# 160 no-operations on TensorE ahead of the first product, and the later ones laid out anew

## The chip, the core and the metric

The kernel runs on one core of one Trainium2 chip. Its five engines are called here PE (TensorE, the matrix products; PEld is its loading of the stationary operand), DVE (VectorE), ACT (ScalarE), POOL (GpSimd) and SP (SyncE, which issues all DMAs). Each works through its own program in order and meets the others at semaphores. The metric is device time in microseconds (us), the median of several executions.

## What is computed

The reference is a causal retention layer followed by a feed-forward layer with softplus:

```
scores = (q @ k.T) / sqrt(64)              # 8 batches, 8 heads, 576 positions, head size 64
ret    = scores * gamma_h ** (i - j)       # for i >= j, else 0
x      = (ret @ v) as 4608 tokens x 512
h      = x @ w_in                          # 512 -> 2048
out    = softplus(h) @ w_out               # 2048 -> 512, all in float32
```

## The kernel before

Retention is done in chunks of 128 tokens and pairs of heads, with a running state between chunks. The feed-forward part takes the tokens in units of 512. Its float32 products are split into high and low parts and are done as three products each, 128x128 by 128x512 ("large products" below). The weights, for the two later passes also some sums of them, pass through a ring of eight buffers that SP fills by DMA.

The program has these stretches on PE.

- **The opening.** PE begins with three products that multiply a tile of ones (`fill`, written by DVE) into a bank that nobody reads (`idle`, L800). Then the retention of the first eight steps is done in an order written out by hand (`BEGIN`): S is the scores of a step (L414), U its sums (L430), V its values (L454), X the part from the state (L462); K and O are DVE's masking and scaling, C the scaling of the values on ACT. SP's first DMAs bring `first` (two parts) and then `whole`, one for each step. The hidden layer's first products stand at L541.
- **The layers' products** (L541, L570, L581, L584, L917, L1053, L1064): large products one behind another, 12 or 6 in a row on one weight block.
- **The chunk runs.** At 33 places between the layers' products `chunk_products` puts the retention of one chunk: up to 128 small 64x64 products, those of scores (L236), sums (L252), values (L340) and states (L352) mixed in a fixed order.

After each chunk run a number is taken from the table `PADS` (its key is the number of the run). `pad()`, called behind each large product of L541, L917 and L1053, then puts out at most `PAD` = 2 no-operations at a time until this number is used up. A no-operation (NOP) reads and writes nothing; its one effect on the program is that all later PE instructions stand that many places further on. PE's instructions come to the core by DMA, in a queue of their own (q8 in the profile).

Of the kernel before, what the change touches and what calls it, by code (L numbers as in the profile page):

```python
# [101 lines left out]
SUM_WORK = ('f2 x3 p4', '', '', 'a0', 'u0 p5', 'u1', '', 'f3', 'p6', 'k0 c0', '', 'v0 v1', 'g0 p7', '', 'g1', '')  # L102
GROUPS = {1: (4, None), 4: (5, 4), 8: (6, 5), 12: (7, 6), 15: (8, 7)}
ODD = 12
PADS = {2: 6, 3: 74, 4: 64, 5: 6, 6: 8, 10: 14, 11: 108, 12: 68, 16: 10, 17: 70, 18: 48, 20: 52, 22: 50, 24: 50, 26: 18, 28: 10, 29: 70, 30: 24}
PAD = 2
LOADS = {1: (10,), 2: (11,), 4: (12, 13), 8: (14, 15), 12: (16, 17), 15: (18, 19)}
SCALES = {3: (10, 11), 7: (12, 13), 11: (14, 15), 14: (16, 17)}
# [14 lines left out]
def retention_softplus_ffn(ctx: ExitStack, tc, first, whole, others, consts, w, out):  # L123
    nc = tc.nc
# [240 lines left out]
    def chunk_products(steps, done, values_first=False):  # L365
# [32 lines left out]
        runs[0] += 1  # L398
        pads[0] = PADS.get(runs[0], 0)

# [395 lines left out]


    idle = ps_val.tile([P, 2, T], F32, tag="val", name="idle")
    for n in range(OPENING):
        nc.tensor.matmul(idle[:, 0, 0:2 * C], fill[:, 0:P], fill[:, 0:2 * C], start=True, stop=True)  # L800

# [637 lines left out]
```

## Time and profile before

| what | value |
|---|---|
| median of 3 runs | 810.11 us (808.95 to 810.88) |
| profiled execution, its own time | 808.12 us |
| profiled execution, span of the trace | 806.4 us |
| PE busy | 799.9 us (99%) |
| PE's share of the chain that ended last | 95% |
| NOPs on PE | 750 |
| PE waits for another engine or a DMA, all rows | 3.4 us |

The time of an execution is the span and some 1.7 us around it. The span runs from the first to the last instruction of any engine. The chain that ended last is the list of work, each piece released by the one before, that leads to the last instruction: an engine that holds 95% of it sets the time, and what the other engines do counts only where PE waits.

### The profile page before, as it was taken

What the parts mean: (1) busy time and instruction counts of PE and PEld (TensorE: products, weight loads), DVE (VectorE), ACT (ScalarE), POOL (GpSimd) and SP (SyncE); (2) the same over time, 40 slices, a digit from 0 to 9 for tenths busy, and PEclk for the clock granted to TensorE, in tenths of its full rate; (3) what the DMA queues carried; (4) which work ended last, traced back from release to release, by engine and by line L of the source; (5) the groups of instructions that cost most, each with busy time, mean ns of one, the idle gap of its engine ahead of it and who ended that gap; (6) DMA issues with size and microseconds to landing.
All of it is one profiled execution on the core that took longest, in us unless ns stands there. A gap on an engine that the chain in (4) does not pass through costs nothing.

```text
span 806.4 us, 19457 instructions
## 1 busy us (share of the span) xinstructions
PE 799.9 (99%) x7292; PEld 659.1 (82%) x7292; DVE 585.9 (73%) x987; ACT 395.3 (49%) x698; POOL 120.9 (15%) x213
## 2 busy tenths in 40 slices
PE   8999999999999999999999999999999999999998
PEld 6788888878888888888888888888888888888887
DVE  5988868788779986777679965546589934335785
ACT  6878763344533363343445654343255734434543
POOL 4322132212221220222111001122100000000000
PEclk9999999999999999999999999999999999999999
DMA  9989989998995779898977678777656675555564
GB/s 359 382 326 318 313 286 363 321 358 294 366 362 209 276 281 384 277 322 263 322 260 234 218 245 256 230 250 252 215 179 215 222 247 195 192 191 194 194 220 158
DMA packets 100457, 216.77 MB, mean 269 GB/s; under 512 B 11152, under 2 KB 11408, under 8 KB 100368
## 3 DMA queue, kind: packets, MB, share of 16 engines
q1 hardware_dynamic: 100368, 215.54, 77.6%
q8 instruction: 61, 1.00, 0.5%
q14 instruction: 28, 0.23, 0.1%
HBM read 174.60 MB, written 40.89 MB: 267 GB/s over the span
## 4 chain that ended last, share of the span: by engine, by line
PE 95%; DVE 2%; DMA 2%; POOL 0%; issue 0%; ACT 0%; SPq 0%; DVEq 0%
PE acc L917 22%; PE sum L1053 20%; PE two L917 14%; PE two L1053 6%; PE y L570 5%; PE h L541 5%; PE y L581 5%; PE third L252 3%; PE acc L1053 2%; PE third L1053 2%; PE y L1053 2%; PE two L236 2%; PE two L340 2%; PE third L917 2%; PE two L352 2%; DMA raw<-whole 1%
## 5 line engine op out<-in xcount | busy, mean ns | idle before, releaser
L917 PE MATMUL acc<-xt,ring 128*128 128x512 f32 x792 | 199.7, 389 | 0.0
L917 PEld LDWEIGHTS acc<-xt,ring 128*128 128x128 f32 x792 | 148.4, 188 | 31.6 <-ACT g L1093 0.3
L1053 PE MATMUL sum<-parts,ring 128*128 128x512 f32 x708 | 170.9, 392 | 0.0
L1047 DVE TENSOR_TENSOR parts<-g,parts 128x512 fp32r<-128x512 f32 x196 | 134.2, 694 | 47.1 <-ACT parts L1043 44.3
L1043 ACT CAST parts<-g 128x512 fp32r<-128x512 f32 x196 | 121.1, 622 | 73.5 <-DVE parts L1047 27.3
L1053 PEld LDWEIGHTS sum<-parts,ring 128*128 128x128 f32 x708 | 131.6, 188 | 27.8
L917 PE MATMUL two<-xt,ring 128*128 128x512 f32 x504 | 128.0, 389 | 0.0
L917 PEld LDWEIGHTS two<-xt,ring 128*128 128x128 f32 x504 | 94.4, 188 | 20.1 <-DVE held L1332 0.4
L1072 ACT ACTIVATE g<-g 128x512 f32<-128x512 f32 x84 | 52.8, 629 | 68.6 <-DVE g L1087 40.4
L1087 DVE TENSOR_TENSOR g<-two,g 128x512 f32<-128x512 f32 x28 | 19.4, 691 | 83.1 <-PE two L917 83.1
L229 POOL TENSOR_TENSOR qv<-qv,consts_sb 128x256 f32<-128x256 f32 x58 | 48.8, 844 | 128.4 <-DMA qv<-others 128.4
L1085 ACT COPY g<-acc 128x512 f32<-128x512 f32 x28 | 16.5, 589 | 95.5 <-PE acc L917 95.5
L1053 PE MATMUL two<-parts,ring 128*128 128x512 f32 x216 | 50.5, 389 | 0.0
L581 PE MATMUL y<-g,wout 128*128 128x512 f32 x192 | 47.6, 395 | 0.0
L1053 PEld LDWEIGHTS two<-parts,ring 128*128 128x128 f32 x216 | 40.5, 188 | 8.5
L541 PE MATMUL h<-xt,win 128*128 128x512 f32 x192 | 46.4, 391 | 0.0
L570 PE MATMUL y<-wout,g 128*128 128x512 f32 x180 | 44.1, 393 | 0.0
L1129 ACT ACTIVATE g<-acc 128x512 f32<-128x512 f32 x28 | 16.7, 597 | 53.3 <-PE acc L917 53.3
L541 PEld LDWEIGHTS h<-xt,win 128*128 128x128 f32 x192 | 35.9, 188 | 8.0 <-DVE win L671 0.4
L581 PEld LDWEIGHTS y<-g,wout 128*128 128x128 f32 x192 | 35.4, 188 | 7.9 <-DVE g L556 0.3
L570 PEld LDWEIGHTS y<-wout,g 128*128 128x128 f32 x180 | 33.3, 188 | 7.4 <-ACT g L552 0.3
L294 DVE TENSOR_TENSOR a<-two,mask 128x512 f32<-128x512 f32 x32 | 22.0, 687 | 20.8 <-PE two L352 17.7
(171 smaller groups left out, 1260.7 us busy)
## 6 DMA issues: line engine op xcount, KB each, us to landing
ring<-split SPq DMA_DIRECT2D x116, 256.0 KB, 4.6
ring<-combined SPq DMA_DIRECT2D x112, 256.0 KB, 3.5
ring<-outcombined SPq DMA_DIRECT2D x112, 256.0 KB, 3.0
ring<-outsplit SPq DMA_DIRECT2D x84, 256.0 KB, 3.4
qv<-others SPq DMA_DIRECT2D x58, 320.0 KB, 4.8
wst<-w SPq DMA_DIRECT2D x32, 512.0 KB, 6.4
keys<-others SPq DMA_DIRECT2D x58, 256.0 KB, 5.0
split<-win SPq DMA_DIRECT2D x16, 512.0 KB, 6.6
```

Of the source, the lines that this page charges most:

```text
L229: nc.gpsimd.tensor_mul(v, v, f.unsqueeze(2).broadcast_to([P, 4, D]))
L252: mm = nc.tensor.matmul(L["T"][rows[h ^ s], t, part[s]], L["kp"][rows[t], s, rows[h]], L["v"][rows[t], s, rows[h]], start=True, stop=True, ...
L294: nc.vector.tensor_mul(a[:, :, at], src.rearrange("p h (s c) -> p h s c", c=HC), mask.unsqueeze(1).unsqueeze(1).broadcast_to([P, 2, 2 * le ...
L541: nc.tensor.matmul(h, tile_of(wins[p], a, kt), xt[:, b, T1 + half, kt % 2], start=(n == 0), stop=(n == 3 * NKT - 1))
L570: nc.tensor.matmul(ys[u][tt], g[:, a, tt * P:(tt + 1) * P], wouts[p][:, :, b], start=p == 0 and n == 0, stop=False)
L581: nc.tensor.matmul(ys[u][tt], tile_of(wouts[p], a, tt), g[:, b], start=u == 1 and p == 2 * MIXED and n == 0, stop=n == 2, skip_group_check ...
L917: nc.tensor.matmul(bank, w[:, ta, kt * P:(kt + 1) * P], xt[:, tb, x, kt], start=start and k == 0, stop=k == 5, skip_group_check=True)
L1043: nc.scalar.copy(t[:, HI], g_slot(J, n))
L1047: nc.vector.tensor_sub(t[:, LO], g_slot(J, n), t[:, HI].bitcast(F32))
L1053: nc.tensor.matmul(bank[m], w[:, a, m * P:(m + 1) * P], t[:, b], start=start and n == 0, stop=n == 2, skip_group_check=True)
L1072: nc.scalar.activation(c, c, AF.Softplus)
L1087: nc.vector.tensor_add(c11, y, c11)
```

## The change

The table `PADS` gets a new key 0 with 160, and `160` NOPs are put out in one unbroken row ahead of the three `idle` products. The entries for the chunk runs are replaced: 750 NOPs behind large products become 964. In all, PE has 1124 instead of 750. Nothing else is changed: products, tiles, waits and the programs of the other engines stay as they are.

```
-PADS = {2: 6, 3: 74, 4: 64, 5: 6, 6: 8, 10: 14, 11: 108, 12: 68, 16: 10, 17: 70, 18: 48, 20: 52, 22: 50, 24: 50, 26: 18, 28: 10, 29: 70, 30: 24}
+PADS = {1: 4, 2: 92, 3: 92, 4: 14, 5: 2, 6: 30, 7: 48, 9: 70, 10: 108, 13: 66, 14: 58, 15: 32, 17: 42, 19: 8, 20: 70, 21: 26, 23: 52, 25: 46, 27: 52, 29: 52, 0: 160}
...
     idle = ps_val.tile([P, 2, T], F32, tag="val", name="idle")
+    for n in range(PADS.get(0, 0)):
+        nc.tensor.nop(hint="pad", nofuse=True)
     for n in range(OPENING):
         nc.tensor.matmul(idle[:, 0, 0:2 * C], fill[:, 0:P], fill[:, 0:2 * C], start=True, stop=True)
```

On PE, at the start of the program, there stood before (`part` is what the DMAs of `first` bring, `raw` what those of `whole` bring; a loading of the stationary operand goes with each product and is not listed):

```order
L1433 UNCONDITIONAL_BRANCH
L800 MATMUL idle<-fill 128x256 x3
L414 MATMUL pair_215<-part_106 64x128 x4
L414 MATMUL pair_215<-part_106 64x64 x4
L430 MATMUL bank<-part_107 64x64 x4
L454 MATMUL bank<-a_whole,part_107 64x128 x4
```

and there stands now:

```order
L1435 UNCONDITIONAL_BRANCH
L800 NO_OP x160
L802 MATMUL idle<-fill 128x256 x3
L414 MATMUL pair_215<-part_106 64x128 x4
L414 MATMUL pair_215<-part_106 64x64 x4
L430 MATMUL bank<-part_107 64x64 x4
L454 MATMUL bank<-a_whole,part_107 64x128 x4
```

All of PE's products now stand behind 160 NOPs, the three on `fill` too.

On PE, behind the second chunk run, the hidden layer's products (`win` is a block of w_in) stood before with six NOPs in three pairs:

```order
L541 MATMUL h<-xt,win_750 128x512
L406 NO_OP x2
L541 MATMUL h<-xt,win_750 128x512
L406 NO_OP x2
L541 MATMUL h<-xt,win_750 128x512
L406 NO_OP x2
L541 MATMUL h<-xt,win_750 128x512 x9
```

and stand now with a pair behind each of them (92 in all after this run); the first of these rows are:

```order
L541 MATMUL h<-xt,win_914 128x512
L406 NO_OP x2
L541 MATMUL h<-xt,win_914 128x512
L406 NO_OP x2
L541 MATMUL h<-xt,win_914 128x512
L406 NO_OP x2
L541 MATMUL h<-xt,win_914 128x512
L406 NO_OP x2
```

The products keep their order; only pairs of NOPs have come between more of them here, and between fewer behind other runs.

## Rows read from the trace of the kernel before

**Rows 1.** The page: span, engines (busy us, share, instructions), instruction queue, chain by engine.

```profile
span 806.4 us, 19457 instructions
...
PE 799.9 (99%) x7292; PEld 659.1 (82%) x7292; DVE 585.9 (73%) x987; ACT 395.3 (49%) x698; POOL 120.9 (15%) x213
...
q8 instruction: 61, 1.00, 0.5%
...
PE 95%; DVE 2%; DMA 2%; POOL 0%; issue 0%; ACT 0%; SPq 0%; DVEq 0%
```

**Rows 2.** Timeline of PE, 0 to 9.5 us: start, length, what, [idle before <-releaser].

```profile
1.53 2.93 PE L800 MATMUL idle<-fill 128*128 128x256 f32 x6 [1.53 <-DVE fill L777]
4.39 0.92 PE L414 MATMUL pair<-part 64*64 64x128 f32 x16
5.47 1.08 PE L430 MATMUL bank<-part 128*64 128x64 f32 x7 [0.16 <-ACT part L232]
...
7.96 0.56 PE L414 MATMUL pair<-raw 64*64 64x128 f32 x16 [0.44 <-DMA raw<-whole]
9.23 0.45 PE L414 MATMUL pair<-raw 64*64 64x128 f32 x8 [0.72 <-DMA raw<-whole]
```

**Rows 3.** Waits of PE, then of PEld: total us, times, longest.

```profile
PE idle L800 <- DVE fill L777: 1.5, 1, 1.5
PE pair L414 <- DMA raw<-whole: 1.2, 2, 0.7
...
PEld pair L414 <- DMA raw<-whole: 2.0, 4, 0.9
```

**Rows 4.** The chain that ended last, to 28 us: start, length, what.

```profile
0.82 0.38 SPq L201
...
2.19 7.00 DMA raw<-whole
9.19 0.04 issue
9.23 0.56 PE pair L414 x16
...
18.44 0.69 DVE win L671
...
25.07 1.87 POOL raw L229 x2
```

**Rows 5.** NOPs of line 406: all; stretches 72.338:72.345 and 72.408:72.415 (same answer but start); 72.33:73.16.

```profile
L406 PEldq NOP  x750: 13/13/13, 48.1 to 552.8; - x188
...
L406 PEldq NOP  x1: 13/13/13, 72.3 to 72.3; - x1
...
L406 PEldq NOP  x1: 13/13/13, 72.4 to 72.4; - x1
...
L406 PEldq NOP  x11: 13/13/13, 72.3 to 73.1; - x11
```

**Rows 6.** The chain that ended last, around 200 us: start, length, what.

```profile
198.48 1.59 PE y L1053 x6
200.07 1.36 PE acc L917 x6
```

**Rows 7.** Four chunk runs as stretches: length, then busy us (instructions) of PE, PEld, DVE, ACT, POOL.

```profile
68.79:70.82 2.03, 2.03 (x130) 1.96 (x129) 1.33 (x4) 1.92 (x4) 0.14 (x1) 1.00 0.96 274
121.78:123.85 2.07, 2.07 (x130) 2.00 (x129) 0.68 (x1) 1.22 (x2) 0.14 (x1) 1.00 1.03 393
320.46:322.58 2.12, 2.12 (x129) 2.04 (x129) 2.12 (x5) 1.12 (x2) 0.14 (x1) 1.00 0.93 337
490.87:493.01 2.14, 2.14 (x129) 2.07 (x128) 0.04 (x1) 1.12 (x2) 0.14 (x1) 1.00 0.68 209
```

**Rows 8.** Timeline of PE, 15 to 36 us: the layers' first products.

```profile
20.75 6.02 PE L541 MATMUL h<-xt,win 128*128 128x512 f32 x24
```

## The prediction, made before the changed kernel ran

> **What bounds the kernel now.** I read the page first, for the engine that sets the time. PE is busy for 99% of the span and holds 95% of the chain that ended last [rows 1]. So a microsecond counts only if PE's stream of products gets shorter or starts earlier or later. The other engines matter where PE waits for them, and there is little of that: the view of waits gives PE 1.5 us for DVE at the very start and 1.2 us, in two pieces, for the DMAs of `whole` in the opening [rows 3]. All large waits in that view belong to other engines.
>
> Second, the timeline of PE over the first 10 us, since 160 of the new NOPs stand there. PE starts its three products on `fill` at 1.53, released by DVE, and the first step's scores at 4.39. It then waits 0.44 and 0.72 us for data of the second and third step [rows 2]. The chain agrees: it comes from the DMA that lands at 9.19, and from 9.23 on it is PE, DVE, ACT and POOL work that hands over to one another, with no DMA in it up to 28 us, where the layers' products take over [rows 4]. So what starts late at 4.39 has a little over one microsecond to spare before the third step, and nothing to be hidden in after that.
>
> **The change part by part.** First, the **160 NOPs ahead of the first product**. PE's sequencer comes to them when the start barrier lets the engines go, at about 0.82, as SP's first issue shows [rows 4]. How long do they take? The trace records 13 ns for each NOP [rows 5], but that is not its price if the next one starts later than that. Two NOPs of one pair, with nothing between them in the program, are recorded in the stretches 72.338 to 72.345 and 72.408 to 72.415 [rows 5]: one starts 0.07 us after the other. Eleven of them start between 72.33 and 73.16, ten steps in some 0.81 us with a load and a product behind every second one: 81 ns for each if load and product are free [rows 5]. So a NOP costs between 13 ns (its own record) and 81 ns. I take 70 ns, because the pair is the nearest case to a row of NOPs: one directly behind another, with the sequencer running ahead of the array (the stretch goes at some 0.16 us for each product, while the large products run at 0.23). That gives 160 x 0.07 = 11.2 us, so the NOPs end at 0.82 + 11.2 = 12.0, and with the pause to the first load the products on `fill` start at about 12.1 instead of 1.53: 10.6 us late.
>
> What hides it? Two things only. DVE's `fill` (until 1.53) is already in this count. Then the two waits for `whole`, 0.44 + 0.72 = 1.16 us, vanish, as all these DMAs have landed by then [rows 2, 3]. PEld waits 2.0 us for the same DMAs [rows 3], but 1.16 of it is what the products lose. What comes after 9.23 is a chain without DMAs [rows 4], and it starts from PE: DVE masks what PE has multiplied, ACT and POOL split it, and DVE and ACT have the conversion of the weights behind these steps in their own programs, so all of it slides with PE. SP's first loads do not slide; those that wait for a freed weight buffer do, and they have that much more slack. So 10.6 - 1.16 = 9.4 us reach the layers' products, and these run without gaps: a row of six takes 1.36 us [rows 6], and no later wait for a DMA is there to take a delay up [rows 3]. A step might find a little more cover, up to the 2.0 us of PEld.
>
> One more thing moves with the NOPs: the first products are slow. The 16 records of the first scores take 0.92 us, the 16 of the second 0.56 [rows 2]. I take this to repeat behind the NOPs, since PE multiplies nothing in them; if not, the three products on `fill` (2.86 us to the next) and the first step would be up to 2 us shorter, and I keep that in the range.
>
> Next, the **pairs behind large products**, 964 for 750. A product with a pair goes through the sequencer in about 0.16 us [rows 5]; the array needs 1.36 / 6 = 0.227 us for it [rows 6]. So the sequencer still gains on the array, 0.07 us with each, and the 214 more cost nothing. The cover is the length of the large products; behind a small product a pair would cost its 0.14 us, but `pad()` is not called there.
>
> Last, **where the blocks of instructions begin**. PE's instructions arrive in 61 packets [rows 1]; 2 x 7292 loads and products and 750 NOPs [rows 1, 5] make some 250 in each, and a chunk run of 128 loads and 128 products [rows 7] is as long as one such block. Does it matter where it is cut? Compare the runs: the usual one takes 2.03 us; three take 2.07, 2.12 and 2.14 [rows 7]; all others, wherever they are cut, are like it or shorter. All that a better layout can win there is 0.04 + 0.09 + 0.11 = 0.24 us. At worst each of the 33 runs becomes like the worst here: 33 x 0.11 = 3.6 us. I take 0: the old layout is near the floor, and a new one is likely to land there too.
>
> [...]
>
> **The sum.** Against the profiled execution: 808.12 + 10.6 - 1.16 + 0 + 0 = 817.5 us. The median of the runs shown is 810.11, which is 1.99 us above that execution; I forecast 810.11 + 9.4 = 819.5 us.
>
> **The rivals.**
>
> *The NOPs hide in the first load (not slower).* If an unbroken row runs at the recorded 13 ns [rows 5], 160 take 2.1 us and end at 2.9; the products on `fill` start 1.4 us late, of which 1.16 vanish in the waits for `whole` [rows 2]: +0.2 us, 810.4. For it: PE is idle until 1.53 and waits twice afterwards, so there is room for some 1.9 us. Against it: no two NOPs in the trace follow each other that closely. It decides below about 23 ns a NOP, where the delay that is left passes 1.6 us. [...]
>
> *The NOPs cost something between,* 25 to 55 ns, if part of the 70 is a change between NOPs and products that a long row saves. At 36 ns they end at 6.6, 5.0 us late, 3.9 in the end: 814.0.
>
> *The layout decides.* If cutting at new places hits every chunk run, 3.6 us come on top: 823. If instead the opening has a pause that the shift removes and the NOPs are hidden as in the first rival, it could win the 0.24 us and what PE waits in the opening, 1.2 us [rows 3]: 808.7, still within what can be measured. To be faster by more, something would have to go that the profile doesn't show.
>
> **How the numbers follow.** A measurement of this kernel can tell about 0.2%, 1.6 us. My forecast, with its own range of 816.5 to 822 (81 ns a NOP gives +11.1; a quick start takes 2 off; the runs before spread by 1 us to either side), gets 0.77. The price between gets 0.08, the hidden NOPs 0.10, a layout that hurts on top 0.02, a gain that I can't see 0.03. Slower is 0.77 + 0.08 + 0.02 = 0.87, same 0.10, faster 0.03. The range reaches down to 814, where the price between ends, and up to 822.
>
> **What would show it.** In the profile of the changed kernel the first product on `fill` starts at about 12.1, no longer released by DVE, with 160 NOPs ahead of it some 70 ns apart; PE's waits for `whole` are gone; the layers' first products (L541, at 20.75 before [rows 8]) start some 9.4 us later, and the shift between the two traces stays the same to the end; the chunk runs take 2.01 to 2.14 us as before. If the products on `fill` start near 3 us, my price for a NOP was wrong. If they start at 12 and the time grows by much less than 9 us, there was cover in the opening that I did not see. If the shift grows along the trace, the layout of the blocks matters more than I hold.

## The result, and the profile after

The changed kernel takes 817.54 us (median of 6 runs, 816.65 to 819.1), the kernel before 809.27 us (6 runs beside it): a ratio of 1.0103, 95% interval 1.0087 to 1.0119, or 8.3 us slower. The profiled execution took 817.83 us (span 816.1), 9.7 us more than that of before. Forecast were 819.5 us and a range from 814 to 822.

The page of the changed kernel, beside [rows 1]:

```profile
span 816.1 us, 19831 instructions
...
PE 798.2 (98%) x7292; PEld 658.0 (81%) x7292; DVE 586.0 (72%) x987; ACT 395.7 (48%) x698; POOL 118.2 (14%) x213
...
q8 instruction: 63, 1.03, 0.5%
...
PE 89%; DMA 5%; DVE 2%; issue 2%; SPq 1%; POOL 0%; ACT 0%; DVEq 0%
```

PE has the same 7292 products and is not busy for longer (798.2 us, before 799.9), yet the span is 9.7 us longer: the time went into PE's idle time. "issue", time in which an engine waited for nothing that the profile shows, now has 2% of the chain. Where it lies is in the timeline of PE, beside [rows 2], and in the rows of the new NOPs (all of them, then those from 0.8 to 6.7 us):

```profile
12.56 2.90 PE L802 MATMUL idle<-fill 128*128 128x256 f32 x6 [12.56 <-issue]
15.39 0.56 PE L414 MATMUL pair<-part 64*64 64x128 f32 x16
15.88 0.45 PE L430 MATMUL bank<-part 128*64 128x64 f32 x8
16.86 0.66 PE L454 MATMUL bank<-a_whole,part 128*64 128x128 f32 x8 [0.52 <-DVE a_whole L421]
17.44 0.90 PE L414 MATMUL pair<-raw 64*64 64x128 f32 x32
```

```profile
L800 PEldq NOP  x160: 13/13/13, 0.9 to 12.5; - x160
...
L800 PEldq NOP  x80: 13/13/13, 0.9 to 6.7; - x80
```

The first product starts at 12.56 instead of 1.53, 11.03 us late, and no longer waits for DVE. The 160 NOPs fill the time from 0.9 to 12.5, 159 steps in 11.6 us: 73 ns each. The trace has most of them 70 or 71 ns apart and every sixteenth about 101.

What reached the layers is in the timeline further on, beside [rows 8]:

```profile
29.22 5.99 PE L541 MATMUL h<-xt,win 128*128 128x512 f32 x24
```

29.22 instead of 20.75: 8.47 us late, so the opening took up 2.56 of the 11.03. Such a figure rests on one execution of each kernel. In two kernels below whose PE instructions in the opening are those of the kernel before, and whose first product also starts at 1.53, the layers' products start at 19.97 and 20.50, so what is taken up is known to some 0.8 us and not to the hundredths that the traces give. The waits of PE over the whole execution, beside [rows 3], and three chunk runs as stretches (the 13th, the 14th and the 26th, beside [rows 7]) show the rest:

```profile
PE idle L802 <- issue: 12.6, 1, 12.6
PE bank L454 <- DVE a_whole L421: 0.7, 2, 0.5
PE acc L919 <- DVE g L1108: 0.6, 1, 0.6
PE two L236 <- DVE g L1118: 0.3, 1, 0.3
PE third L252 <- DMA keys<-others: 0.3, 1, 0.3
```

```profile
234.68:237.25 2.57, 2.26 (x130) 2.08 (x129) 1.20 (x2) 1.62 (x3) 0.14 (x1) 1.00 0.96 316
245.63:248.01 2.38, 2.25 (x113) 2.04 (x112) 1.42 (x3) 1.53 (x4) 0.69 (x2) 1.00 1.03 382
500.69:502.72 2.03, 2.03 (x130) 1.96 (x129) 0.04 (x1) 1.12 (x2) 0.14 (x1) 1.00 0.77 199
```

The waits for `whole` are gone. In this execution 1.5 us more come between 180 and 250 us: PE waits for DVE at L919; in the 13th chunk run its wait is put down to the DMA of the keys, and in the 14th the wait of PEld is put down to POOL's scaling of the values, which had itself waited for their DMA. The 26th run, one of the three long ones before, now takes the usual 2.03. After 250 us the difference between the traces stays between 9.7 and 10.0; the 18th and the 26th run, 0.1 us shorter each, take 0.2 back.

### The profile page after: what moved, and what is told of

The parts are those of the page before. It is cut to its first block, busy times and chain, and to the rows that moved or that the text cites. A ratio compares the mean times of both kernels' runs of the same rounds, so it can differ in the third digit from the quotient of the medians.

```text
span 816.1 us, 19831 instructions
## 1 busy us (share of the span) xinstructions
PE 798.2 (98%) x7292; PEld 658.0 (81%) x7292; DVE 586.0 (72%) x987; ACT 395.7 (48%) x698; POOL 118.2 (14%) x213
## 4 chain that ended last, share of the span: by engine, by line
PE 89%; DMA 5%; DVE 2%; issue 2%; SPq 1%; POOL 0%; ACT 0%; DVEq 0%
PE sum L1055 20%; PE acc L919 19%; PE two L919 13%; PE two L1055 6%; PE y L570 5%; PE h L541 5%; PE y L581 5%; PE third L252 2%; PE acc L1055 2%; PE third L1055 2%; PE two L236 2%; DMA outcombined<-quad 2%; PE two L340 2%; PE third L919 2%; PE two L352 2%
## 5 line engine op out<-in xcount | busy, mean ns | idle before, releaser
L919 PE MATMUL acc<-xt,ring 128*128 128x512 f32 x792 | 199.8, 390 | 0.6 <-DVE g L1108 0.6
L919 PEld LDWEIGHTS acc<-xt,ring 128*128 128x128 f32 x792 | 148.4, 188 | 32.3 <-DVE g L1108 1.1
L919 PE MATMUL two<-xt,ring 128*128 128x512 f32 x504 | 128.1, 389 | 0.0
L919 PEld LDWEIGHTS two<-xt,ring 128*128 128x128 f32 x504 | 94.5, 188 | 20.1 <-DVE held L1334 0.4
L229 POOL TENSOR_TENSOR qv<-qv,consts_sb 128x256 f32<-128x256 f32 x58 | 46.5, 802 | 128.6 <-DMA qv<-others 128.5
```

Of the source, the lines that this page charges most:

```text
L229: nc.gpsimd.tensor_mul(v, v, f.unsqueeze(2).broadcast_to([P, 4, D]))
L919: nc.tensor.matmul(bank, w[:, ta, kt * P:(kt + 1) * P], xt[:, tb, x, kt], start=start and k == 0, stop=k == 5, skip_group_check=True)
```

## Experiments

All times stand against runs of the kernel before on the same chip.

### The layout without the front row, the front row without the layout

```
-PADS = {1: 4, 2: 92, ..., 29: 52, 0: 160}
+PADS = {1: 4, 2: 92, ..., 29: 52}
```

> The new table without its key 0: no NOPs ahead of the first product, 964 behind large products. All chunk runs are thus cut 160 instructions further on than in the changed kernel. My theory (the front row costs by its time, the cuts are worth little): the time of the kernel before within 0.3%, so about 809 us, and in the trace the layers' products start within 0.3 us of before. Rival (the cuts decide): chunk runs 0.1 to 0.5 us longer at many places, up to 3.6 us more, about 813 us.

Measured: 811.26 us against 808.71, ratio 1.0036 (1.0019 to 1.0053). The layers' products start at 19.97, so the opening was even a little shorter. The 2.5 us come from behind it, and the waits of PE name no engine for them:

```profile
PE idle L802 <- DVE fill L777: 1.5, 1, 1.5
PE y L570 <- issue: 1.5, 1, 1.5
PE pair L414 <- DMA raw<-whole: 1.2, 2, 0.8
PE two L352 <- issue: 1.2, 2, 0.8
```

The measured 2.5 us lie between the theory's figure (up to 2.4 us) and the rival's (about 4), and the interval (1.5 to 4.3 us) reaches both: the places of the cuts cost something. That the opening was 0.78 us shorter, with the same PE instructions in it, neither side had foreseen. The other half:

```
-PADS = {1: 4, 2: 92, ..., 29: 52, 0: 160}
+PADS = {2: 6, 3: 74, ..., 30: 24, 0: 160}     # the old table and the front row
```

> The old table plus the 160 NOPs ahead of the first product: the front row alone, the chunk runs cut 160 instructions away from where the kernel before has them. My theory: as late as the changed kernel, +8.3 to +9.7 us, about 817.5 us, the layers' products late by 8.5 us. Rival (the new table gives back or costs something): over 1 us away from the changed kernel, in either direction, seen as longer or shorter chunk runs.

Measured: 824.24 us, ratio 1.0188 (1.0151 to 1.0225), 15.5 us slower, almost twice the change itself. The first product starts at 12.56 as in the changed kernel, the layers' products at 29.54. So the front row costs what it did there, and the rival holds for the rest: the old table, shifted by 160, loses some 7 us more (15.5 against 8.3; 5.5 between the two profiled executions). More than half of that is one place. Waits of PE, then its timeline in the twelfth chunk run and behind it, then the run and the 3.42 us after it as stretches (the third number from the end is PEclk):

```profile
PE third L252 <- issue: 2.6, 1, 2.6
PE acc L919 <- issue: 1.2, 1, 1.2
```

```profile
221.43 0.22 PE L352 MATMUL two<-qv,sx 64*64 64x64 f32 x1
224.25 0.27 PE L252 MATMUL third<-qv,keys 64*64 64x64 f32 x1 [2.60 <-issue]
...
224.56 2.87 PE L1055 MATMUL y<-parts,ring 128*128 128x512 f32 x6
```

```profile
220.10:224.98 4.88, 2.28 (x117) 2.08 (x109) 0.29 (x1) 0.80 (x2) 0.41 (x2) 0.97 1.03 408
224.98:228.40 3.42, 3.42 (x10) 2.61 (x10) 3.37 (x6) 0.00 (x0) 1.42 (x3) 0.55 0.87 341
```

The run takes 4.88 us for the usual 2.03. In its middle PE waits 2.60 us for nothing that the profile shows. A packet of the instruction queue q8 starts at 221.91, after PE has stopped, and ends at 222.91; PE goes on 1.34 us later. In the nine waits of this kind of 0.2 us and more in these two kernels and in the one without NOPs below, PE goes on 1.28 to 1.60 us after such a packet has ended. That PE waits there for its own instructions is read from this, and borne out by the cut that is moved below. Behind the wait the products are slow as well: in the next 3.42 us the granted clock was 0.55, and six products take 2.87 us where they took 1.59 behind another run before [rows 6].

### The same NOPs where they are hidden

```
-    for n in range(PADS.get(0, 0)):
-        nc.tensor.nop(hint="pad", nofuse=True)
...
-    runs, pads = [0], [0]
+    runs, pads = [0], [PADS.get(0, 0)]      # used up behind L541 and L570, ahead of the second chunk run
...
+                if p < 3:                   # behind the products of L570
+                    pad()
```

> The same 1124 NOPs and the new table, but the 160 stand in pairs behind the large products of the hidden and output layers ahead of the second chunk run, instead of ahead of the first product; from the second chunk run on every instruction stands where the changed kernel has it. My theory: NOPs are free there, so the time of the kernel before, 809 us within 0.3%, first product at 1.5 us, and chunk runs 2 to 33 as in the changed kernel but without its late start. Rival (the new places of the instructions themselves cost the time): 817 us as the changed kernel.

Measured: 808.79 us against 808.71, ratio 1.0004 (0.9993 to 1.0015). With the same 1124 NOPs, and every instruction from the second chunk run on at the place that it has in the changed kernel, the 8.3 us are gone. The 374 NOPs that this kernel has more than the one before, all behind large products, are free, and the new table, at the places for which it was made, costs and brings nothing that can be measured (0.6 us less to 1.2 us more by the interval). (The start of the layers' products, 22.18 in the profiled execution, has another reason, in the last section.)

### A late first product without NOPs

```
-    nc.vector.memset(fill, 1.0)
+    for _ in range(22):
+        nc.vector.memset(fill, 1.0)
```

> The kernel before, without any new NOP, but DVE writes the tile of ones 22 times instead of once, so that PE's first product is let go at about 12.5 us by DVE instead of 1.53. My theory (a late first product costs it, whatever makes it late): the layers' products late by 8 to 9 us, +8 to +10 us, about 818 us. Rival (NOPs or shifted instruction blocks cost it): the time of the kernel before, 809 us.

Measured: 821.17 us, ratio 1.0163 (1.0136 to 1.0189), 12.5 us slower. The 22 writes took longer than I had reckoned, so the delay is larger than in the changed kernel:

```profile
15.36 2.93 PE L801 MATMUL idle<-fill 128*128 128x256 f32 x6 [15.36 <-DVE fill L778]
18.21 0.92 PE L414 MATMUL pair<-part 64*64 64x128 f32 x16
32.36 6.03 PE L541 MATMUL h<-xt,win 128*128 128x512 f32 x24
```

First product 13.83 us late, layers' products 11.61: 2.22 are taken up, as with the NOPs. No instruction of PE has been shifted here. So the delay itself is the cost, whoever makes it; the rival falls. (In the profiled execution one wait for instructions, 0.66 us in the 26th chunk run, is also in the time. PE's instructions are those of the kernel before, where that run has no such wait.)

### How many NOPs are free

The kernel of the third experiment with 24 or 64 of the 160 put ahead of the first product, the rest behind the early large products:

```
+    for n in range(24):                     # 64 in the other
+        nc.tensor.nop(hint="pad", nofuse=True)
...
+    runs, pads = [0], [PADS.get(0, 0) - 24]
```

> As the run with the 160 NOPs moved, but 24 of them stand ahead of the first product and 136 behind the large products before the second chunk run; from there on every instruction stands where the changed kernel has it. At 72 ns a NOP the first product starts at 0.90 + 24 x 0.072 + 0.06 = 2.7 us, 1.2 us late. My theory (the waits for the first loads cover 1.2 us and more): the time of the kernel before within 0.2%. Rival (no cover, each NOP costs its 72 ns): +1.2 us or more, and the chain of waits no longer begins with the DMA of the third step.

> The same with 64 NOPs ahead and 96 moved. First product at 0.90 + 64 x 0.072 + 0.06 = 5.6 us, 4.0 us late. My theory: 1.2 us covered by the waits for data and up to 1.4 us more by the first steps running faster, so the layers' products late by 1.5 to 2.9 us and the time +1.5 to +2.9 us, about 811 us. Rival (the time goes with the shift of the instructions, which is the same as with 24 or none): the time of the kernel before.

And 256 NOPs in front, with the old table: a whole block of instructions by my estimate. It comes from the packets of q8, which number 58 without any NOP, 61 with 750, 62 with 910, 964 or 1006 and 63 with 1124; with the 14584 loads and products these are 249 to 251 instructions a packet, and PE's few others come on top:

```
+PADS = {2: 6, 3: 74, ..., 30: 24, 0: 256}
```

> The old table and 256 NOPs ahead of the first product: one whole block of instructions, so that every later instruction keeps its place in its block. First product at 0.90 + 256 x 0.072 + 0.06 = 19.4 us, 17.9 us late. My theory (late start by the number of NOPs, stalls by the place in the block): layers' products late by 15.4 us, chunk runs as in the kernel before, +15 to +17 us, about 825 us. Rival (any shift of the instructions makes chunk runs stall as 160 did with the old table, some 6 us more): about 831 us.

The starts of the first products and of the layers' products, in order with 24, 64 and 256 NOPs ahead:

```profile
2.68 2.90 PE L804 MATMUL idle<-fill 128*128 128x256 f32 x6 [2.68 <-DVE pair L790]
...
20.75 6.01 PE L541 MATMUL h<-xt,win 128*128 128x512 f32 x24
```

```profile
5.59 2.90 PE L804 MATMUL idle<-fill 128*128 128x256 f32 x6 [5.59 <-issue]
...
22.56 5.99 PE L541 MATMUL h<-xt,win 128*128 128x512 f32 x24
```

```profile
19.77 2.90 PE L802 MATMUL idle<-fill 128*128 128x256 f32 x6 [19.77 <-issue]
...
36.52 5.99 PE L541 MATMUL h<-xt,win 128*128 128x512 f32 x24
```

| NOPs ahead | first product late by | layers' products late by | taken up | time against before (95% interval) |
|---|---|---|---|---|
| 24 | 1.15 | 0.00 | 1.15 | 0.9988 (0.9976 to 1.0001) |
| 64 | 4.06 | 1.81 | 2.25 | 1.0023 (1.0008 to 1.0038) |
| 160 (the change) | 11.03 | 8.47 | 2.56 | 1.0103 (1.0087 to 1.0119) |
| 256, old table | 18.24 | 15.77 | 2.47 | 1.0204 (1.0171 to 1.0237) |

With 24 NOPs the delay is covered whole. (The profile puts that start down to `pair`, which DVE had finished at 2.52; the last of the NOPs starts at 2.6.) With more, the cover is 2.2 to 2.6 us, and every further NOP puts the first product off by its 73 to 75 ns. With 256 the time is 16.9 us up (13.8 to 19.2 by the interval), close to 15.77 and short of the some 22 that stalls as with the old table shifted by 160 would give; PE has no wait for "issue" behind its first product. Shifted by these 256, one packet more (62 for 61), the old table works again.

### No pads at all, and one cut moved

```
-PADS = {2: 6, 3: 74, ...}
+PADS = {}
```

> The kernel before with an empty table: no NOP anywhere, the chunk runs cut wherever they fall. Theory drawn from the first experiments (a chunk run that needs the next block of instructions while it is still being fetched waits for it): some runs wait 0.4 to 2.9 us, each wait ending some 1.3 us after a fetch has ended, in all +3 to +20 us, start of the layers' products as before. Rival (my step before the runs: the cuts are worth 0.24 us): within 0.3% of the kernel before.

Measured: 809.2 us against 809.25, ratio 1.0005 (0.999 to 1.002). My theory drawn from the first runs falls here: without any pad there is one long wait for instructions, in the sixth chunk run ("issue" 1.1 below), and all other runs are as short as ever. So a layout that nobody has placed need not cost anything: this one does not, while the old table shifted by 160 lost some 7 us and the new one without its front row 2.5.

```profile
PE idle L800 <- DVE fill L777: 1.5, 1, 1.5
PE third L252 <- issue: 1.1, 1, 1.1
PE pair L414 <- DMA raw<-whole: 1.1, 2, 0.7
```

Then the kernel with the 160 in front and the old table, with the cut of its twelfth run moved by 40 instructions:

```
-..., 10: 14, 11: 108, 12: 68, ..., 0: 160}
+..., 10: 54, 11: 108, 12: 28, ..., 0: 160}
```

> The kernel with 160 NOPs in front and the old table, with 40 NOPs taken from behind the twelfth chunk run and put behind the tenth: runs 11 and 12 are cut 40 instructions further on, all others stay. In that kernel run 12 waited 2.86 us for a block of instructions and the products behind it ran at half the clock. My theory (the place of the cut in that one run decides): both go, 4.5 us less than that kernel, about 819.7 us, run 12 at 2.03 us. Rival (that run waited by chance, for data or because the DMAs were full): no difference, about 824 us, or another run waits in its place.

Measured: 820.95 us, ratio 1.0144 (1.0122 to 1.0165), 3.3 us less than without the move, though the intervals of the two ratios overlap. Run 12 takes 3.36 us instead of 4.88 and the clock stays up behind it (1.00 in the 3 us that follow). Its wait, now 1.02 us, stands 20 products earlier in the program than the wait of 2.60 us did: 40 instructions with their loads, just as far as the cut has moved. So the wait belongs to the cut. But it did not go, and the rival's other half came true in part: other places wait in its stead. The waits of PE, beside those above:

```profile
PE acc L919 <- issue: 2.7, 3, 1.4
PE third L252 <- issue: 1.0, 1, 1.0
```

In all they are 3.7 us, as without the move (3.8); the 1.5 us between the two profiled executions are about what the lower clock had cost behind run 12. The longest wait at L919, 1.41 us, stands before a product that waits 0.14 us without the move, with the same number of instructions ahead of it. And runs that are cut at the same count of instructions in the kernel before don't wait at all. So whether PE waits at a cut depends on more than the count, and what that is stays open.

### The three products on the tile of ones

```
-OPENING = 3
+OPENING = 0        # 5 in the last run; 0 once in the changed kernel, once in the kernel before
```

> The changed kernel without the three products on the tile of ones (they go into a bank that nobody reads). They stand in the late path, 2.83 us from their start to the first scores. Theory that they pay for themselves (the first steps then begin at the slow rate): the layers' products earlier by 1 us or less. Rival (what comes behind does not depend on them): earlier by the whole 2.8 us, about 814.7 us.

> The kernel before without those three products. The first scores may then start when the first load has landed, before 4.39. My theory (the third step's load, landing at 9.2 us, sets the time up to there; only the speed of the steps counts): same within 0.2%, or up to 1 us slower as the first steps run slower for longer. Rival (the first product's time counts): up to 1 us faster.

> The kernel before with five products on the tile of ones instead of three: first scores 1.7 us later at the slow rate, of which 1.2 us are covered by the waits for the second and third step's data. My theory: same within 0.2% (0.5 us late if the rate rises at the same time as before, less if it rises earlier). Rival (no cover): 1.7 us slower.

These leave out or add products into a bank that nobody reads. Measured: without them the changed kernel takes 815.56 us, ratio 1.0085 (1.0069 to 1.0101), some 1.5 to 2 us less than the change, with intervals that overlap. The trace is clearer:

```profile
12.67 0.92 PE L414 MATMUL pair<-part 64*64 64x128 f32 x16 [12.67 <-issue]
13.52 0.70 PE L430 MATMUL bank<-part 128*64 128x64 f32 x8
...
15.55 1.56 PE L414 MATMUL pair<-raw 64*64 64x128 f32 x32
...
27.92 5.98 PE L541 MATMUL h<-xt,win 128*128 128x512 f32 x24
```

The first scores start at 12.67 instead of 15.39 and the layers' products at 27.92 instead of 29.22: of 2.72 us, 1.30 are kept, half of what was dropped. So the three products stand in the late path and pay back about half. What they pay back is the rate of the first steps: in the changed kernel the first scores take 0.56 us, the sums 0.45 and the next 32 records of scores 0.90, without the three products 0.92, 0.70 and 1.56. In the kernel before, leaving them out changes nothing in the medians (809.43 us, 1.0005, 0.9995 to 1.0015), and five of them give 808.47 us, 0.9987 (0.9974 to 0.9999), too little to be called a gain where twelve kernels stand beside the one before. No run gave a kernel that beats the one before by more than can be told.

## Why the prediction was right, step by step

- **The price of a NOP** held. Taken from one pair 0.07 us apart [rows 5]: 70 ns; measured 73 in the row of 160, since every sixteenth step takes about 101. The first product was 11.03 us late, forecast 10.6. The 13 ns of the NOP's own record fall, and the rival with them: 64 NOPs, which would be covered at that price, cost 1.9 us by the ratio. No two NOPs in the row start less than 70 ns apart. That is the price of a NOP and not of every instruction: a chunk run takes 2.03 us for 128 loads and 128 products [rows 7], 8 ns an instruction.
- **That nothing after the opening takes the delay up** held: 8.47 us late at the layers' first products, 8.3 us in the medians. The sign that the shift stays the same to the end did not: in the profiled execution it grows to 9.7 to 10.0, by waits for data and not by the layout.
- **The cover in the opening** was mis-sized: 1.16 us forecast, 2.56 measured (2.2 to 2.6 in the experiments). I had counted only PE's waits for `whole`. Another 1.08 us are in the first step. From the first to the second scores it takes 7.96 - 4.39 - 0.44 = 3.13 us before, without the wait for `whole` [rows 2], and 17.44 - 15.39 = 2.05 now. Two things could shorten it. One I read past in the rows: before, the first sums wait 0.16 us for ACT and each of them for a piece of its scaling, which waits for the second part of `first` (1.08 us for seven of them [rows 2], 0.45 for all eight now). The other is the slow rate of the first products, which I took to repeat behind the NOPs. The run without the three products on `fill` tells them apart: there the scaling is long done and the first step runs at the slow rate throughout, in 15.55 - 12.67 = 2.88 us. So ACT's scaling is worth some 0.25 us and the rate some 0.83. The rate is the larger term, and I had put it at nothing and kept it as a bound. The three products on `fill` are as slow as before (2.83 us to the next), but the first scores behind them are not. In that same run, where the slow rate does repeat, the first scores are 8.28 us later than before and the layers' products 7.17: 1.11 us are taken up, what I forecast. Where the rate rises differs between executions: with the old table and 160 in front the first scores took 0.92 again and the layers' products were 0.3 us later. The last 0.3 us of the 2.56 lie in the later steps and are within what openings differ by.
- **The pairs behind large products** cost nothing, as forecast: moving 160 more there gave 1.0004.
- **The layout** at 0 held for this change, but its bound did not. I took 0.11 us a run as the worst. A single run took 2.85 us too long, with a granted clock of 0.55 in the 3.42 us behind it, and a table off by 160 lost some 7 us. The step that failed is the reading of [rows 7] as a scale: one execution of one layout shows the waits that it happened to have. With the same PE instructions the 26th run takes 2.14 us there and 2.95 in the kernel with the late tile. That the old table kept its cuts at good places on purpose is likely but not shown, as no pads at all cost nothing. Had the new table been as wrong for its places as the old one shifted by 160, the time would have passed the upper end of the range (824.24).

The forecast was 9.4 us: 0.4 too little for the start and 1.4 too little for the cover make it 8.4, and the medians show 8.3 (7.0 to 9.6 by the interval). That they agree so closely is in part luck, as openings alone differ by 0.8 us. The 1.5 us of waits behind the opening are in the difference of the two profiled executions, 9.7 us, and not in that of the medians. The profiled execution of before was 1.15 us faster than the median of the six runs of the kernel before; whether its slower executions have such waits is not shown.

## What to carry to other kernels

Read the price of an instruction that does nothing from the distance to the next one's start (73 ns in the row of 160) and not from its recorded length (13 ns). It was free behind the large products (ratio 1.0004), where by the estimate in the prediction the sequencer gains 0.07 us on the array with each. Work put ahead of the first product was covered by the waits and the slow rate of the first steps, here some 2.3 us (24 NOPs wholly), and by nothing later. A bound read from one arrangement that does well is no bound; test it by shifting the arrangement.

## What the runs showed of the hardware

Two things about the granted clock were not expected. It fell where PE had waited 2.60 us in a chunk run (0.55 in the next 3.42 us, above). Behind the other waits for instructions in these runs, 1.51 us and less, no lower clock is recorded. And it fell in one opening: in the profiled execution with the 160 moved, PE was busy for 1.93 of 3.40 us, the next stretch was granted 0.50, and the layers' products started 1.43 us later than before, with the first product at the same 1.53 and the third step's scores at 9.24 (before 9.23). The two stretches (third number from the end: PEclk):

```profile
5.50:8.90 3.40, 1.93 (x32) 1.46 (x32) 1.53 (x4) 1.43 (x7) 0.40 (x1) 1.00 1.01 404
8.90:12.30 3.40, 3.06 (x48) 2.61 (x48) 1.74 (x4) 2.63 (x11) 0.74 (x1) 0.50 1.03 417
```

The kernel's median is that of the kernel before and this execution is the slowest of its ten, so it does not happen in all. What sets it off is not shown: the kernel before was busy for 1.33 of the 2.44 us from 7.56 to 10.00 and has no lower clock behind them. The slow rate of the first products is read from their durations: 0.92 us for 16 scores and 0.69 for eight sums also stand in the stretch that was granted 0.50, but at the start of the traces themselves no lower clock is recorded. Open are the waits for data between 180 and 250 us: in some profiled executions they are 1 us and more (the change, the moved 160, the late tile), with 24 NOPs 0.5. Which transfers decide that was not tried.
